# Norms and casts of three batches on ScalarE or GpSimd, one matmul for each filler, and a new order of all operations

## The chip, the core and the metric

One Trainium2 chip, one of its eight cores. The core has five engines that run side by side, each with its own queue of instructions in program order: TensorE (PE; its weight loads are listed as PEld), VectorE (DVE), ScalarE (ACT), GpSimd (POOL) and SyncE (SP, which here only issues DMAs). They wait for one another through semaphores. The metric is the time of one execution on the device in microseconds (us), from the first to the last instruction; less is better.

## What is computed

Attention with a forget gate over 8 batches of 8 heads, 576 positions of 64 dimensions, followed by a bilinear feed-forward network (FFN) on all 4608 tokens:

```python
scores = (q @ k.T) / 8 + cum[:, None] - cum[None, :]      # cum = cumsum(log(clip(f, 1e-4, 1)))
scores[above the diagonal] = -1e9
attn = softmax(scores); x = attn @ v                       # for each of 64 heads
x = heads side by side                                     # 4608 x 512
out = ((x @ w_a) * (x @ w_b)) @ w_out                      # 512 -> 1536 -> 512
```

Inputs and output are float32; the kernel works in float16 with float32 sums.

## The kernel before

The kernel is written as a list of 2311 operations, made by calls of `op` (L124). Each operation has a number, the letters of the engines that may run it (E for TensorE, D, A, P, S for VectorE, ScalarE, GpSimd and SyncE), and what it depends on. Two long constants at the end of the kernel then settle everything: `ORDER` names the operations in the order in which they are issued, and `CHOICE` gives one letter to each operation that has a choice, in the order in which the operations were made. `laid_out` joins the two and a loop issues them. Nothing is rearranged after that: each engine runs its part of `ORDER` first in, first out. Where an operation takes a buffer, it takes the next of a ring (`RING`, L100), and has to wait until the last user of that buffer has finished.

**Attention.** Work is cut into 32 pairs of heads, t = 0 to 31, four to a batch; u = t // 2 names two pairs that share their score matmuls. Inputs are loaded by SyncE (`load_qk` L280, `load_v` L267) in float32, cast to float16 (`cast_qk` L290, kind `caqk`; `cast_v` L275, kind `cav`) and, for q and k, transposed by VectorE (`tqk`, L302). For batch 0 the casts may run on ScalarE, GpSimd or VectorE; for the later batches they run on GpSimd. For a pair and each block of 128 queries i = 0 to 4 (the last has 64), the steps are:

- scores on TensorE (`qk_group` L389). For batches 0 to 2 the decay and the mask come out of further matmuls there, so that
- VectorE takes the maximum of a row straight from PSUM (`do_max` L483, kinds `max0` to `max4`); from batch 3 on it adds the decay and takes the maximum in one instruction (`do_decay`, L512);
- ScalarE takes the exponential, with the row's sum (`do_exp` L539, `exp0` to `exp4`);
- VectorE takes the reciprocal of the sum (`rec`, L554);
- GpSimd multiplies the block of P by it (`do_norm` L561, `norm0` to `norm4`, in place: 128, 256, 384, 512 and 576 columns); all norms are on GpSimd;
- P is transposed: for batch 0 by TensorE (`ptr` L585, evicted by `evp`), from batch 1 on by DMA transposes that SyncE issues (`tr`, L579), in three parts for a pair of batch 1: A0 (i = 0 and 1), A1 (i = 2) and B (i = 3 and 4);
- TensorE multiplies with v (`pve`, `pv`, `pv4`) and ScalarE or VectorE evicts the result to x (`eve`, `ev`, `ev4`).

**The decay.** The cumulative sums are made at the start: VectorE scans them (`fscan`), splits them into a high and a low half (`fhi`, VectorE or ScalarE; `flo`, VectorE or GpSimd), and TensorE and an eviction (`crep`, `cev`) spread them to rows for the score matmuls.

**FFN.** It runs on tiles of tokens: 0, 256 and 512 with 256 tokens each, 768 with 384, then six of 512 and one of 384. A tile needs x of its tokens: those of 0 and 256 need batch 0 only, that of 512 needs batch 1 too (its first 192 rows), that of 768 the rest of it. For each of 12 blocks there are a product with w_a (`psa`), one with w_b (`psb`), four matmuls each (L874), a copy of the first to float16 (`aev`, ScalarE or VectorE) and the product of both on VectorE (`mul`, L890); then w_out (`pso`, L899), a copy (`ocopy`) and the store (`sto`, L914). FFN matmuls are put between those of attention by `ORDER`.

**Weights.** GpSimd issues seven loads that cast on the way (`weights` L355, kind `ldw`, L365). Operation 89 is the first 512 columns of w_a, 90 the same of w_b, 91 the other 1024 columns of w_a, 92 those of w_b, 93 to 95 are w_out. Blocks 4 to 11 of a tile need 91 and 92.

**Fillers.** 40 operations (`filler` L175, numbers 2 to 41) multiply the identity with itself into an unused PSUM buffer of the ring `ff`; they compute nothing. One is four matmuls of 128 columns. 31 of them stand ahead of the first FFN matmul in `ORDER`, nine behind it, none behind the matmuls of token 512 on.

**The end.** The last 128 tokens are stored in two halves, which ScalarE's queue issues; the output's copies go through a ring of two buffers.

Of the kernel before, what the change touches and what calls it, by code (L numbers as in the profile page):

```python
# [37 lines left out]
def kernel(  # L38
# [136 lines left out]
    def filler(_):  # L175
        p = ps.tile([128, 512], FP32, tag="ff", bufs=RING["ff"], name="idle")
        for n in range(4):
            nc.tensor.matmul(out=p[:, 128 * n:128 * n + 128], lhsT=ident, rhs=ident, start=True, stop=True)
# [126 lines left out]
    def batch_inputs(b):  # L305
# [4 lines left out]
        for which, part, gm in items:  # L310
            gate = qk_ops[(2 * (b - 1) + gm // 4, gm % 4)][-1:] if b >= EARLY else []
            if which == "v":
# [4 lines left out]
                ca = op(("P" if 0 in part else "APD") if b == 0 else "P", "cav", lambda e, part=part: cast_v(e, b, part), [ld, o_p], 512 * m)  # L317
# [15 lines left out]
            for lo, hi in (((0, 5), (5, TW)) if b == 0 else ((0, TW),)):  # L333
                ca = op("APD" if b == 0 else "P", "caqk",
# [226 lines left out]
    def do_norm(e, t, i, h):  # L561
        st = T[("st", t)]
        if i == 4:
            p, c = p_blocks(t, 4), 28
        else:
            p, c = p_blocks(t, i)[:, :, h, :], 20 + 2 * i + h
        ENG[e].tensor_scalar(out=p, in0=p, scalar1=st[:, c:c + 1], scalar2=1.0, op0=MUL, op1=MUL)  # L567
# [97 lines left out]
    def softmax(t, g, qk, sc, rows, st_users, pu, norms):  # L665
# [4 lines left out]
        for i in groups[g]:  # L670
# [308 lines left out]
    for t0, n in [(0, 256), (256, 256), (512, 256), (768, 384)] + [(1152 + 512 * n, 512 if n < 6 else 384) for n in range(7)]:  # L979
# [3 lines left out]
        42-44 0 20 41 2 1 64 26 31 23 54 55 45 16 32 13 12 71 46 37 47 56 18 67 27 65 34 72 73 68 48 24 19  # L983
# [3 lines left out]
        142 6 154 155 92 147 143 159 149 91 148 144 160 162 161 108 166-168 145 172 131 52 53 132 179 173 14  # L987
# [4 lines left out]
        310 305 1610 1612 246 214 247 158 226 215 227 311 234 189 1611 235 157 222 449 1614-1616 1613 283  # L992
        312 340 195 294 1617 223 1618 1620 228 229 341 1619 347 1621 236 342 450 94 343 191 232 288 1622 349
        260 237 233 1623 242 348 282 300 1624 366 211 344 1625 240 261 243 241 95 373 1626-1628 367 190 197
        1629 1630 1632 1631 196 302 1633 248 249 374 375 301 368 369 1634-1636 350 1638 284 262 263 392 1637
# [5 lines left out]
        1667 1670 455 1671-1673 1676 1677 421 388 382 381 389 456 1674 401 333 1678 357 413 1675 364 1679  # L1001
# [3 lines left out]
        465 460 500 409 463 505 1703 416 1704 480-482 424 508 440 428 422 1705 1706 509 471 477 483 479 510  # L1005
# [130 lines left out]
```

## Time and profile before

| | us |
|---|---|
| median of 3 runs | 400.67 |
| lowest, highest | 399.65, 400.86 |
| span of the profiled execution | 400.7 |
| first FFN matmul (tile 0) | 30.37 |
| first FFN matmul of tile 512 | 95.58 |
| first FFN matmul of tile 768 | 119.79 |

The busy time of an engine is that in which one of its instructions runs. A matmul's end is modelled in the profile, so that a busy TensorE need not be at its peak. Waits are put down to what came last before the engine went on. In the timeline a row gives start, length, engine, line and operation, what is written and read with its shape, and in square brackets the engine's idle time just before and what ended it. In the groups a row gives a line, the operation and shape, its count, then the busy time of all, the mean of one in nanoseconds, and the idle time ahead of them. In the list of DMA issues the last number is the time from the issue to the landing in us. In the list of waits the three numbers are total us, times and the longest.

### The profile page before, as it was taken

To read this page: it belongs to the slowest core of one execution; us is meant where nothing else is said; L and a number is where in the kernel's file an instruction comes from. 1 tells how busy PE (TensorE), PEld (TensorE's weight loads), DVE (VectorE), ACT (ScalarE), POOL (GpSimd) and SP (SyncE) were. 2 spreads that over 40 slices of the span, in tenths; PEclk is the share of its full clock that TensorE was granted. 3 is DMA by queue.
4 is the path that set the end of the run, shared out by engine and by line. 5 is a ranking of instruction groups with operands and counts; after the bars stand their busy time and mean duration, and the time that the engine had idled before them with its cause. 6 is when DMAs were issued, how large, how long until landed. Compare 5 with 4: busy or idle time off the path is not lost.

```text
span 400.7 us, 11076 instructions
## 1 busy us (share of the span) xinstructions
PE 383.2 (96%) x4040; PEld 212.0 (53%) x4040; DVE 315.3 (79%) x907; ACT 250.0 (62%) x757; POOL 253.6 (63%) x424
## 2 busy tenths in 40 slices
PE   8598799998999999999999999999999999999996
PEld 7466576765855544454445454544444444444553
DVE  8989798976778988997988889898969892373560
ACT  5798766666667778758785777577868673300011
POOL 3889876887397876897896849787968553000000
PEclk9889999998999999999999999999999999999999
DMA  7999989989999999999999999999997729000102
GB/s 282 240 186 289 204 177 224 213 150 215 208 301 208 227 171 330 201 277 212 295 187 286 211 255 273 233 241 190 276 187 218 157 66 202 28 2 36 71 0 79
DMA packets 148311, 78.22 MB, mean 195 GB/s; under 512 B 130592, under 2 KB 133408, under 8 KB 148256
## 3 DMA queue, kind: packets, MB, share of 16 engines
q1 hardware_dynamic: 144272, 72.53, 77.4%
q0 software_dynamic: 3696, 4.72, 7.0%
q8 instruction: 31, 0.51, 0.5%
q10 hardware_dynamic: 288, 0.26, 0.2%
q14 instruction: 24, 0.20, 0.1%
HBM read 49.69 MB, written 9.58 MB: 148 GB/s over the span
## 4 chain that ended last, share of the span: by engine, by line
PE 79%; DMA 9%; DVE 4%; POOL 2%; ACT 2%; issue 2%; SPq 0%; POOLq 0%; DVEq 0%; ACTq 0%
PE pso L899 22%; PE psa L874 22%; PE psb L874 21%; PE sc L401 8%; DMA wa<-in_moe_w_a_dram 5%; PE pv L611 2%; DVE st L488 2%; DMA k<-in_k_dram 1%; PE pv L613 1%; PE sc L636 1%; DMA PTB<-spread 1%; DMA PTB<-PB 1%; DVE qT L302 1%; PE pv L623 1%; ACT PB L550 1%
## 5 line engine op out<-in xcount | busy, mean ns | idle before, releaser
L874 PE MATMUL psa<-xT,wa 128*128 128x512 f16 (+2 forms) x528 | 116.2, 343 | 2.3 <-DMA wa<-in_moe_w_a_dram 1.7
L874 PE MATMUL psb<-xT,wb 128*128 128x512 f16 (+2 forms) x528 | 116.2, 343 | 0.1
L899 PE MATMUL pso<-wout,ht 128*128 128x512 f16 (+1 forms) x444 | 98.4, 374 | 0.0
L567 POOL TENSOR_SCALAR PA<-PA,st 128x128 f16<-128x128 f16 (+2 forms) x162 | 76.0, 482 | 31.8 <-DVE st L559 20.4
L890 DVE TENSOR_TENSOR ht<-psb,a 128x512 f16<-128x512 f32 (+2 forms) x132 | 76.2, 589 | 22.0 <-PE psb L874 15.0
L512 DVE CUSTOM_DVE_ANT_0 S<-sc,spread 128x128 f32<-128x128 f32 (+3 forms) x160 | 86.7, 567 | 7.7 <-PE sc L401 5.4
L138 ACT CAST a<-psa 128x512 f16<-128x512 f32 (+2 forms) x85 | 43.5, 515 | 55.9 <-PE psa L874 53.8
L874 PEld LDWEIGHTS <-wa 128*128 128x128 f16 x528 | 50.1, 99 | 45.5 <-issue 3.7
L874 PEld LDWEIGHTS <-wb 128*128 128x128 f16 x528 | 50.4, 99 | 41.5 <-issue 1.7
L567 POOL TENSOR_SCALAR PB<-PB,st 128x512 f16<-128x512 f16 (+1 forms) x84 | 58.7, 712 | 15.7 <-DVE st L559 14.6
L550 ACT ACTIVATE PA<-S,st 128x256 f16<-128x256 f32 (+2 forms) x120 | 59.9, 502 | 12.5 <-DVE st L512 12.4
L899 PEld LDWEIGHTS <-ht 128*128 128x128 f16 x444 | 41.7, 98 | 46.8 <-issue 1.3
L488 DVE TENSOR_REDUCE st<-sc 128x2 f32<-128x512 f32 (+7 forms) x68 | 46.3, 723 | 6.0 <-PE sc L401 5.3
L401 PE MATMUL sc<-kT,qT 32*128 32x128 f16 (+5 forms) x960 | 41.7, 272 | 5.5 <-ACT PA L550 2.1
L550 ACT ACTIVATE PB<-S,st 128x512 f16<-128x512 f32 x40 | 28.5, 714 | 7.9 <-DVE st L512 7.9
L401 PEld LDWEIGHTS <-qT 32*128 32x128 f16 (+1 forms) x960 | 18.6, 96 | 26.7 <-issue 14.4
L142 DVE CAST a<-psa 128x512 f16<-128x512 f32 (+2 forms) x47 | 26.2, 560 | 7.2 <-PE psa L874 6.6
L559 DVE RECIPROCAL st<-st 128x2 f32<-128x2 f32 x128 | 18.5, 157 | 14.0 <-ACT PA L550 8.7
L142 POOL CAST k<-k 128x1152 f16<-128x1152 f32 (+1 forms) x15 | 20.5, 1367 | 8.9 <-DMA k<-in_k_dram 8.9
L138 ACT COPY osb<-pso 128x512 f32<-128x512 f32 (+1 forms) x22 | 12.4, 570 | 19.9 <-PE pso L899 15.1
L138 ACT CAST xT<-pv 128x512 f16<-128x512 f32 (+2 forms) x39 | 17.0, 446 | 11.8 <-PE pv L636 5.8
L140 POOL TENSOR_SCALAR q<-q 128x1152 f16<-128x1152 f32 (+1 forms) x15 | 20.6, 1372 | 5.0 <-DMA q<-in_q_dram 4.2
(98 smaller groups left out, 491.5 us busy)
## 6 DMA issues: line engine op xcount, KB each, us to landing
spread<-cum_d SPq DMA_DIRECT2D x20, 576.0 KB, 5.9
out_dram<-osb SPq DMA_DIRECT2D x35, 256.0 KB, 3.8
q<-in_q_dram SPq DMA_DIRECT2D x15, 576.0 KB, 7.3
k<-in_k_dram SPq DMA_DIRECT2D x15, 576.0 KB, 5.2
v<-in_v_dram SPq DMA_DIRECT2D x32, 256.0 KB, 6.1
wout<-in_moe_w_out_dram POOLq DMA_DIRECT2D x3, 512.0 KB, 8.7
v<-in_v_dram SPq DMA_DIRECT2D x8, 128.0 KB, 7.2
wb<-in_moe_w_b_dram POOLq DMA_DIRECT2D x1, 1024.0 KB, 13.5
```

What stands on the lines that cost most here:

```text
L138: nc.scalar.copy(out=out_, in_=in_)
L140: ENG[e].tensor_scalar(out=out_, in0=in_, scalar1=0.125, scalar2=1.0, op0=MUL, op1=MUL)
L142: ENG[e].tensor_copy(out=out_, in_=in_)
L401: nc.tensor.matmul(out=dst, lhsT=lhsT, rhs=rhs, start=start, stop=stop, skip_group_check=True)
L488: nc.vector.tensor_reduce(out=m if i == 4 else st[:, 2 * i:2 * i + 2][:, h:h + 1] if isinstance(x, list) else m, in_=y, axis=AXX, op=MAX, ...
L512: nc.vector.tensor_tensor_reduce(out=o, in0=x, in1=y, scale=-1.0, scalar=3e38, op0=ADD, op1=MIN, accum_out=m)
L550: nc.scalar.activation(out=p_blocks(t, i)[:, :, h, :], in_=x.rearrange("p (j k) -> p j k", k=128), func=EXP, scale=sign, bias=st[:, c:c + ...
L559: nc.vector.reciprocal(out=st[:, 20 + 2 * i:22 + 2 * i], in_=st[:, 10 + 2 * i:12 + 2 * i])
L567: ENG[e].tensor_scalar(out=p, in0=p, scalar1=st[:, c:c + 1], scalar2=1.0, op0=MUL, op1=MUL)
L874: nc.tensor.matmul(out=o, lhsT=w16[:, db, 128 * fb:128 * fb + 128], rhs=tokens(db, t0, n), start=(db == 0), stop=(db == 3))
L890: nc.vector.tensor_tensor(out=ht[:, 0:n], in0=T.pop(("psb", t0, fb))[:, 0:n], in1=T.pop(("a16", t0, fb))[:, 0:n], op=MUL)
L899: nc.tensor.matmul(out=o, lhsT=T[("ht", t0, fb)][:, 128 * tb:128 * tb + 128], rhs=wout16[:, fb, c], start=(fb == 0), stop=(fb == 11))
```

## The change

Four edits. A filler is one matmul of 512 columns, with the identity repeated four times as the moving operand. Casts of q, k and v of batches 1 to 3 may run on ScalarE or GpSimd. Norms of batches 0 to 2 may run on ScalarE or GpSimd; on ScalarE a norm is an activation with the function Copy, the reciprocal being its scale for each partition. `ORDER` and `CHOICE` are replaced as a whole.

```diff
     def filler(_):
         p = ps.tile([128, 512], FP32, tag="ff", bufs=RING["ff"], name="idle")
-        for n in range(4):
-            nc.tensor.matmul(out=p[:, 128 * n:128 * n + 128], lhsT=ident, rhs=ident, start=True, stop=True)
+        nc.tensor.matmul(out=p.rearrange("p (n k) -> p n k", n=4), lhsT=ident,
+                         rhs=ident.unsqueeze(1).to_broadcast([128, 4, 128]), start=True, stop=True)
...
-                ca = op(("P" if 0 in part else "APD") if b == 0 else "P", "cav", lambda e, part=part: cast_v(e, b, part), [ld, o_p], 512 * m)
+                ca = op(("P" if 0 in part else "APD") if b == 0 else "PA" if b < 4 else "P", "cav", lambda e, part=part: cast_v(e, b, part), [ld, o_p], 512 * m)
...
-                ca = op("APD" if b == 0 else "P", "caqk",
+                ca = op("APD" if b == 0 else "PA" if b < 4 else "P", "caqk",
...
-        ENG[e].tensor_scalar(out=p, in0=p, scalar1=st[:, c:c + 1], scalar2=1.0, op0=MUL, op1=MUL)
+        if e == "A":
+            nc.scalar.activation(out=p, in_=p, func=COPY, scale=st[:, c:c + 1])
+        else:
+            ENG[e].tensor_scalar(out=p, in0=p, scalar1=st[:, c:c + 1], scalar2=1.0, op0=MUL, op1=MUL)
...
-                nm = op("P", f"norm{i}", lambda e, i=i, h=h: do_norm(e, t, i, h), [rc])
+                nm = op("PA" if b < 3 else "P", f"norm{i}", lambda e, i=i, h=h: do_norm(e, t, i, h), [rc])
...
     ORDER = """
-        42-44 0 20 41 2 1 64 26 31 23 54 55 45 16 32 13 12 71 46 37 47 56 18 67 27 65 34 72 73 68 48 24 19
...
+        0 16 7 9 31 21 28 17 3 42 43 6 15 12 5 32 10 1 71 18 66 72 64 44 54 55 45-48 65 26 67 25 49 50 13 56
...
+        390 437 481 313 1709 38 326 320 39 508 384 287 41 36 29 426 471 427 428 431 482 483 412 509 424
...
+        2281 2285-2288 2291 2292 2289 2290 2282 2293-2303 2306-2310 2304 2305 35
     """
     CHOICE = """
-        DPAADDAAPPAPAAPADPADDAAADADDDDDAADDDDAAADAAADDAAAADAAAAADAAAAAAADAAAAAADDAAADADADDAAAAAADDAAAAAAAAA
...
+        DPADAPAAPPAPAPAAPPPPPAPPPPPPPPPPPPPPPPPPPPPPPPPPAPAPPAPDDADADDDADAAAADADADAADAADDDPPPPPPPPAPPPPPPPP
...
```

Given out to the operations, the letters and the order come to this (kinds that differ):

| | before | after |
|---|---|---|
| norms of batches 0, 1, 2 on ScalarE (of 36 each) | 0, 0, 0 | 4, 10, 17 |
| casts of later inputs on ScalarE | 0 | 1 (v of batch 2) |
| casts of batch 0 on ScalarE, GpSimd, VectorE | 5, 5, 1 | 4, 7, 0 |
| `flo` on VectorE, GpSimd | 1, 1 | 0, 2 |
| `fhi` on VectorE, ScalarE | 2, 0 | 1, 1 |
| `cev` on VectorE, ScalarE | 0, 4 | 1, 3 |
| FFN copies `aev` on VectorE, ScalarE | 47, 85 | 54, 78 |
| output copies `ocopy` on VectorE, ScalarE | 15, 22 | 12, 25 |
| evictions `evp` of transposes on VectorE, ScalarE | 11, 5 | 8, 8 |
| evictions `eve`, `ev`, `ev4` on VectorE, ScalarE | 18, 54 | 24, 48 |
| GpSimd's weight loads, in order | 89, 90, 92, 91, 93, 94, 95 | 90, 89, 91, 92, 93, 94, 95 |
| fillers ahead of the first FFN matmul, behind it | 31, 9 | 29, 11 |
| the last two stores | ScalarE | SyncE, the halves swapped |

After, the memsets `pad` are GpSimd's first work behind the identity. Between the loads 91 and 92 GpSimd has seven norms of batch 0 (132, 145, 127, 102, 108, 133, 126) and a cast of k of batch 1 (273). The five fillers 38, 39, 41, 36 and 29 stand in a row on TensorE's queue, ahead of the products with v of batch 1 (426, 431, 424, 415), which stand ahead of the matmuls of tile 512. One filler (35) is TensorE's last instruction.

More of the change, by code (lines that the diff above doesn't have):

```diff
@@ new lines @@
+        472 442 1732 1733 495 444 445 513 385 405 430 433 434 500 435 436 521 522 528 540 443 1734-1736 568
+        478 1738 1739 541 542 507 709 506 512 526 1737 1740 485 524 1742 569 574-576 525 461 1741 1744 546
+        548 1743 1746-1749 577 579 578 1745 1750 1751 1754 1755 1752 1753 1758 1759 1756 1757 1760 547 549
+        463 523 543 545 570 571 529 532 572 551 573 527 533 534 603 536 537 1761-1764 580-582 552 554 550
+        1708 11 535 553 604 605 555 556 1765 1713 530 600 601 531 538 616 558 559 583 585 584 586 587 1767
@@ new lines @@
+        602 1768-1770 618 557 544 619 539 562 1772 1774 563 620 1773 1776 622 560 590 1778 564 565 1777 1779
+        591 588 566 1775 710 1780 1782 1781 1783-1787 561 592 593 589 611 594 598 626 595 623 671 638 678
+        645 640 647 624 673 1788 679 1789 646 1790 648 1791 1792 1794 1793 1796 1797 639 1795 672 641 642
+        596 680 1798 674 675 567 1800 1802 1801 612 1804 1799 1803 649 650 597 627 630 681 682 684 599 631
+        606 634 1806 608 632 635 685-687 676 651 1805 1807 652 633 653 1808 643 1809 1812 607 617 1810 1811
@@ new lines @@
+        688-690 1814 636 692 1766 644 1813 1815-1817 693 1818 609 654-656 1820 712 614 659 660 657 658 683
+        661 1821 628 629 1819 610 637 694 677 625 621 662 697-699 714 1822 700 691 664 665 695 1825 1826 701
+        801 798 1827 1830 1831 1828 667 613 706 716 615 1771 666 668 728 730 1832 713 761 704 763 762 799
+        1833 764 768 1835 1837 769 1836 736 1838 735 1829 1839-1842 702 800 737 1843 696 770 1844 703 729
+        1847 707 771 772 1845 669 738 721 1823 670 663 731 802 739 705 717 722 724 741 765 767 803 720 732
@@ new lines @@
+        1892 856 842 1895 1896 904 855 814 1898-1900 831 1903 1904 860 861 866-868 897 896 898 1887 899 901
+        914 959 966 900 1907 1905 815 960 961 968 1901 1908 1911 907 926 933 934 902 1909 903 1913 1912 1915
+        928 936 1910 935 1917 1916 997 1919 908 813 967 927 1906 905 919 969 998 962 1918 963 915 918 922
+        937-939 929 1014 970 972 930 932 1015 916 917 1921 923 940 973-975 1914 1004 1005 965 1920 942 941
+        1922 971 964 1923 1924 1007 1927 1925 1926 943 1002 944 946 976 977 924 931 1018 947 948 945 1929
@@ L1091 @@
+        PAAAPPPPPAAAAAPPPPPPPPAPPPAAADDDAADDADPPAPPPPPAPAPPAAAPAPPPPAAPAADDAPPPAPPAPAPAAPPAAAPPPPPPPADAAAAAA
+        AAAAAAADAAAADAAAAADDDAAAAADDADAADAAAADADDADDAADDDADDAAADAADDDDAAADADDAADDADDADADADDADDAADDAADDAAAAAA
+        DAADAAADDAAAAAAAAAADAAAAAAADADAADADAAADAAAAAAADAAAAAAADDAAAAAADADADAAAADDDDDAADADDDADDAAADDAADDDDAAA
+        AAAASDS
     """
```

82 lines of the change are left out of this document (45 added, 37 removed), and 102 rows, old and new, of the table ORDER.

## The prediction

> **What bounds the kernel now.** First the summary of the profile: span, busy time of each engine. Then the busy time by stage, for the places where an engine is not full; then the chain of waits inside those.
>
> ```profile
> span 400.7 us, 11076 instructions
> PE 383.2 (96%) x4040; PEld 212.0 (53%) x4040; DVE 315.3 (79%) x907; ACT 250.0 (62%) x757; POOL 253.6 (63%) x424
> ```
>
> ```profile
> 10.00:45.00 35.00, 25.96 (x493) 19.75 (x490) 31.51 (x77) 27.83 (x99) 31.03 (x53) 0.90 1.08 236
> 45.00:80.00 35.00, 34.14 (x589) 25.11 (x587) 32.55 (x72) 24.44 (x79) 26.01 (x42) 1.00 1.04 202
> 80.00:97.00 17.00, 15.22 (x242) 9.88 (x240) 11.98 (x29) 11.11 (x41) 13.85 (x25) 0.96 0.94 168
> 97.00:120.00 23.00, 22.55 (x340) 15.68 (x339) 15.89 (x37) 14.12 (x48) 14.49 (x24) 0.95 1.11 255
> 120.00:397.00 277.00, 276.95 (x2307) 134.35 (x2306) 215.12 (x671) 166.31 (x485) 164.56 (x274) 1.00 0.78 184
> ```
>
> The columns of the stages are stretch, length, busy PE, PEld, DVE, ACT, POOL, then granted clock and DMA share. From 120 us on TensorE is busy 276.95 of 277 us: there the end is set by TensorE's work alone, which the change does not alter. What can be gained or lost lies before 120 us. From 10 to 80 us VectorE is the fullest engine (64.06 of 70 us, 91.5%); from 80 to 97 us no engine is full, and something is waited for in turn.
>
> ```profile
> 84.49 1.80 DVE st L488 x2
> 87.65 0.46 POOL q L140
> 88.98 1.08 POOL PA L567 x3
> 90.06 4.18 DMA PTB<-spread
> ```
>
> ```profile
> 94.28 0.35 PE L636 MATMUL pv<-PTB,nv 128*64 128x64 f16 x10 [1.77 <-DMA PTB<-spread]
> 95.58 0.93 PE L874 MATMUL psa<-xT,wa 128*128 128x256 f16 x4
> ```
>
> The chain there runs through GpSimd's queue (norms, a cast of a later q between them), then a DMA transpose, then values of batch 1, and only then (95.58) the first FFN matmul of tokens 512 on, which need batch 1. Up to there TensorE has only the FFN of 512 tokens to fill in, and has used it up. So the time is: the moment of that matmul, plus work that is the same in both kernels. At the start nothing of the FFN is ready, and VectorE leads.
>
> The profiled execution's span, 400.7 us, equals the median of the three runs (400.67), so sums against the one hold for the other. A measurement of this kernel can tell about 0.3% (1.2 us) from no change.
>
> **The change, part by part.** Handing the letters of CHOICE to the operations in turn gives: 31 norms of batches 0 to 2 go from GpSimd to ScalarE (4, 10 and 17 by batch), one cast of v (batch 2) too; VectorE loses one cast of q, its subtraction `flo` and one of its `fhi` casts; everything else is order.
>
> *Start.* VectorE's queue loses three instructions before the second pair of scores, which ScalarE and GpSimd take:
>
> ```profile
> 6.99 0.49 DVE L142 CAST wout<-cum_f 32x256 f16<-32x256 f32 x2
> 7.52 1.03 DVE L220 TENSOR_TENSOR wout<-cum_f,wout 32x320 f16<-32x320 f32 x1
> 12.65 1.16 DVE L140 TENSOR_SCALAR q<-wout 128x512 f16<-128x512 f32 x1
> ```
>
> ```profile
> L138 ACT CAST xT<-rows 128x320 f16<-128x320 f32 (+1 forms) x4 | 1.6, 396 | 1.0 <-PE rows L225 1.0
> 5.54 0.86 POOL L140 TENSOR_SCALAR q<-q 128x640 f16<-128x640 f32 x1 [4.23 <-DMA q<-in_q_dram]
> ```
>
> 1.03 + 1.16 + half of 0.49 = 2.4 us, less one eviction of rows (`cev`) that it gains, about the 0.4 that ScalarE takes for one: 2.0 us off the leading queue. GpSimd has room for them, since its memsets (`pad`, L169) move into its 4.23 us of idle time before 5.54. So batch 0 may run 2.0 us early.
>
> *Weights.* Against this stand the weight loads. Before, the two large ones are issued one behind the other:
>
> ```profile
> 21.71 0.81 POOL L365 DMA_DIRECT2D wb<-in_moe_w_b_dram  x1
> 22.51 0.75 POOL L365 DMA_DIRECT2D wa<-in_moe_w_a_dram  x1
> ```
>
> ```profile
> wb<-in_moe_w_b_dram POOLq DMA_DIRECT2D x1, 1024.0 KB, 13.5
> wa<-in_moe_w_a_dram POOLq DMA_DIRECT2D x1, 1024.0 KB, 21.7
> ```
>
> ```profile
> 44.21 0.61 PE L874 MATMUL psa<-xT,wa 128*128 128x256 f16 x4 [1.65 <-DMA wa<-in_moe_w_a_dram]
> 45.37 0.42 DVE L890 TENSOR_TENSOR ht<-psb,a 128x256 f16<-128x256 f32 x1 [1.81 <-ACT a L138]
> ```
>
> They land at 35.2 and 44.2, 9.0 us apart: one queue, one after the other. TensorE waits 1.65 us for the second, and VectorE 1.81 behind it. After, `wa` goes first, then seven norms and a cast of k (1.4 us), then `wb`:
>
> ```profile
> L567 POOL TENSOR_SCALAR PA<-PA,st 128x128 f16<-128x128 f16 x54 | 20.0, 376 | 15.8 <-DVE st L559 10.0 <-ACT a L138 2.6 <-issue 2.3
> L567 POOL TENSOR_SCALAR PA<-PA,st 128x256 f16<-128x256 f16 x54 | 25.7, 482 | 6.9 <-DVE st L559 4.9 <-issue 1.8
> L142 POOL CAST k<-k 128x1152 f16<-128x1152 f32 x14 | 19.6, 1398 | 8.0 <-DMA k<-in_k_dram 8.0
> ```
>
> Four norms at 0.376, three at 0.482 and the cast make 4.3 us. By GpSimd's queue `wa` is issued at about 21, so it lands at 34.5 (estimate: 21 + 13.5), and `wb`, issued at about 26, follows at 43.5 (34.5 + 9.0): 0.7 before the second one landed until now. TensorE and VectorE reach it sooner and wait longer. So of the 2.0 us only some 0.9 are left at the first product that needs it (45.37). Bounds: -2.0, if it lands as soon as it is needed, to +3, if it starts only after its issue and takes the 21.7 of the slower row. Taken: **-0.9**, by the row of 9.0.
>
> *From 45 to 97 us.* VectorE's content between that product and the first of token 512 comes to the same within 0.3 us, counted off both orders with the durations of this trace (it evicts three transposes and two outputs less, but has taken over scores of batch 1 from the time before). It is busy 32.55 + 11.98 = 44.5 of 52 us. At the 91.5% that it reaches from 10 to 80 us this takes 48.7: 3.3 less. That needs GpSimd not to be late again; and of its 39.9 busy us here, 17 norms go away before the first FFN copy of token 512: 3, 4, 5, 2 and 3 of 128, 256, 384, 512 and 576 columns.
>
> ```profile
> L567 POOL TENSOR_SCALAR PA<-PA,st 128x384 f16<-128x384 f16 x54 | 31.5, 589 | 9.1 <-DVE st L559 5.6 <-ACT PA L550 1.8 <-DVE st L557 1.7
> L567 POOL TENSOR_SCALAR PB<-PB,st 128x512 f16<-128x512 f16 x56 | 38.2, 694 | 11.6 <-DVE st L559 11.3
> L567 POOL TENSOR_SCALAR PB<-PB,st 128x576 f16<-128x576 f16 x28 | 20.9, 748 | 4.2 <-DVE st L559 3.3 <-ACT PB L550 0.6
> L550 ACT ACTIVATE PA<-S,st 128x256 f16<-128x256 f32 x40 | 20.0, 501 | 4.1 <-DVE st L512 4.1
> L550 ACT ACTIVATE PB<-S,st 128x512 f16<-128x512 f32 x40 | 28.5, 714 | 7.9 <-DVE st L512 7.9
> L142 POOL CAST nv<-v 128x1024 f16<-128x1024 f32 x16 | 16.6, 1038 | 2.7 <-PE pv L613 1.8 <-DMA v<-in_v_dram 0.9
> ```
>
> That is 1.1 + 1.9 + 2.9 + 1.4 + 2.2 = 9.6 us; no ScalarE norm is in the trace, but ScalarE's activations of those widths take as long (501 and 714 ns), so it gains the same 9.6, plus 1.0 for the cast, beside 63.4 busy us of the 87 from 10 to 97 us: 74, or 85%. It has room, if the waits do not grow. The DMA transposes keep their 4 us each. Bounds: 0 to -7.5 (all idle time of VectorE); taken **-2.7**, short of 3.3 because transposes and loads, with the DMA engines full (share 0.94 to 1.08), end some of these waits too.
>
> *Clock.* After the wait of 1.77 us the granted clock fell:
>
> ```profile
> 90.00:95.00 5.00, 3.23 (x66) 1.77 (x64) 4.62 (x8) 2.33 (x7) 5.00 (x10) 1.00 1.06 215
> 95.00:100.00 5.00, 5.00 (x42) 3.65 (x38) 1.51 (x5) 3.98 (x12) 2.10 (x4) 0.66 1.08 210
> ```
>
> A mean of 0.66 over 5 us is 3.4 us at half clock, 1.7 us lost. The new order puts five fillers in a row just ahead of those values of batch 1. Bounds 0 and -1.7; taken **-0.9**, as the wait itself may stay.
>
> The Trainium skill ("TensorE: Matmul & The Clock Gate", Why this matters for your kernels) sets the limit at idle gaps over about 3 us. By that rule nothing would be gained here, the sum being 0.9 higher, still in the forecast's case; the row shows a drop after 1.77 us. Its window of 3413 ns (same page, Part 1) is what the row gives.
>
> *Fillers.* Four matmuls become one; the columns stay 512. Ten run after the first FFN matmul instead of nine, another after all stores; the trace has 14.9 us for 160, so four cost 0.37:
>
> ```profile
> L178 PE MATMUL idle<-ident 128*128 128x128 f16 x160 | 14.9, 257 | 1.7 <-POOL ident masks.py:199 1.4 <-ACT spread L550 0.4
> ```
>
> Two of them fall into the full stage: +0.2 at most with the rest hidden in waits (0 to 0.7).
>
> *End.* The last two stores move from ScalarE's queue to SyncE's, in swapped order, so the one whose copy is last waits behind the other's issue:
>
> ```profile
> 397.59 0.37 ACT L138 COPY osb<-pso 128x256 f32<-128x256 f32 x1 [2.22 <-DMA out_dram<-osb]
> 397.99 0.34 ACTq L914 DMA_DIRECT2D out_dram<-osb  x1
> ```
>
> One issue is 0.34: **+0.2** (0 to 0.4). From 120 to 397 us VectorE takes seven more FFN copies; it is busy 215 of 277 there, which covers them.
>
> **Sum:** 400.7 - 0.9 - 2.7 - 0.9 + 0.2 + 0.2 = **396.6 us**.
>
> **Rivals.**
> - *Nearly all idle time goes.* Start -2.0, middle -5, clock -1.7: 392.4 with the two small costs. For it: the idle time is there on every engine from 80 to 97 us. Against: weights and transposes stay. 17%.
> - *The front stays where it was.* If the DMA engines set the pace (share 1.04 to 1.08 up to 80 us, and the chain passes through a DMA of 4.18 us), the loads and transposes end the waits as before: start -0.9, nothing else, 400.2. 16%.
> - *ScalarE becomes the wait (slower).* A norm on ScalarE waits for the reciprocal, and exponentials of the next scores queue behind it; VectorE's next reciprocals wait for those.
>
> ```profile
> ACT PA L550 <- DVE st L488: 3.7, 3, 1.4
> ACT spread L550 <- DVE st L488: 3.1, 3, 1.8
> ```
>
>   Between 10 and 95 us ScalarE waits for VectorE 1.1 us at a time (6.8 in 6). If each of 17 norms brought that, 18.7 us would be added where the 87 - 74 = 13 us are free: the first FFN matmul of token 512 comes 5.7 us late against ScalarE's room, and with -2.0 from the start the end is at 404.4. It decides from a mean wait of 0.76 us. Against: the norms stand some places behind their reciprocals. 15%. The Trainium skill (same page, opening table) calls ScalarE's queue strictly first in, first out; the waits shown agree.
>
> **How the numbers follow.** The forecast's case (394 to 399) has 52%, and its own edges reach the neighbours. Faster by over 0.3% (below 399.5): forecast 52 + 17, with 1 of the second rival: 70%. Within 0.3%: 15%. Slower (above 401.9): 15%. The range runs from 391.0 (first rival with its bounds) to 402.5 (half of the third): it leaves out about 5% below and 13% above.
>
> **What would show it.** Right: the first FFN matmul of token 512 near 91.5 instead of 95.58; no half clock around it; VectorE above 80% busy from 80 us to there; a wait for `wb` near 40 us longer than 1.65; TensorE full from about 115 us. Wrong: ScalarE at 90% or more with VectorE's reciprocals waiting for it; new TensorE waits after 120 us, which the sum puts at nothing; a `wb` landing after 45.

## The result, and the profile after

| | before | after |
|---|---|---|
| median, us | 400.16 (4 runs, 399.11 to 400.86) | 412.87 (4 runs, 411.25 to 414.06) |
| ratio | 1 | 1.0292, 95% interval 1.0234 to 1.0350 |
| span of the profiled execution, us | 400.7 | 409.5 |
| first FFN matmul of tiles 0, 256, 512, 768 | 30.37, 66.27, 95.58, 119.79 | 29.7, 64.9, 92.06, 116.8 |

The changed kernel is 2.9% slower by the ratio in the table (the two medians alone give 3.2%); 396.6 was predicted. The medians below are over all runs, and the ratios leave out three runs in a slower state of the chip: one of the filler alone, and two of the last kernel with mixed queues, whose median is 480.6 without them. The spans of the two profiled executions lie 8.8 us apart, the medians 12.7. A run's time is 1.8 us above its span (411.25 and 409.5), so the profile of after is that of its fastest run, and that of before of an execution some 2 us above its median. What follows explains the 8.8 us that the two traces hold.

The summary of the profile of after (span, then busy time of each engine, its share and count):

```profile
span 409.5 us, 10797 instructions
PE 387.0 (95%) x3920; PEld 205.5 (50%) x3920; DVE 314.4 (77%) x912; ACT 264.6 (65%) x781; POOL 237.7 (58%) x395
```

Its busy time by stage, in the stages of before (stretch, length, PE, PEld, DVE, ACT, POOL, clock, DMA share, GB/s):

```profile
10.00:45.00 35.00, 29.40 (x483) 18.62 (x483) 30.79 (x75) 29.51 (x101) 25.84 (x42) 0.85 1.05 226
45.00:80.00 35.00, 34.32 (x542) 25.51 (x541) 30.96 (x75) 31.53 (x90) 23.35 (x35) 1.00 0.86 176
80.00:97.00 17.00, 15.77 (x249) 10.25 (x249) 13.61 (x35) 14.86 (x46) 11.29 (x18) 1.00 1.04 191
97.00:120.00 23.00, 22.05 (x347) 14.65 (x342) 16.94 (x41) 16.48 (x52) 9.78 (x16) 1.00 1.07 238
```

```profile
120.00:409.00 289.00, 278.01 (x2292) 133.87 (x2289) 214.79 (x668) 165.78 (x485) 161.13 (x269) 1.00 0.77 182
```

The front does what was forecast: the norms' move shows (GpSimd 26.01 to 23.35 us from 45 to 80, ScalarE 24.44 to 31.53), and the clock is full from 80 to 120 us. (From 10 to 45 us it is 0.85 against 0.90; kernels here that share the first 896 operations of before have 0.80 to 0.90 there, so the difference is not clear of that spread.) The loss is behind 120 us: TensorE, busy for 276.95 of 277 us before, is now idle for 11.0 of 289, 3.0 of them behind its last matmul, which the window of before leaves out. The first two of the five entries in the list of its waits from 120 us on (total, times, longest; the same view of before has no entry at all):

```profile
PE sc L639 <- DMA PTB<-PB: 5.7, 8, 1.1
PE psa L877 <- DVE ht L893: 0.7, 1, 0.7
```

It waits mostly for the DMA transposes of P, the last step of a pair's softmax, ahead of `pv4`. Call a round the time from the first scores (`qk0`) of two pairs to those of the next two. Nine rounds lie between the `qk0` of pairs 12 and 13 and that of pairs 30 and 31. The window between those two moments, first before, then after:

```profile
123.13:310.91 187.78, 187.73 (x1721) 89.42 (x1721) 165.75 (x554) 138.06 (x412) 147.05 (x244) 1.00 1.00 236
```

```profile
122.10:320.20 198.10, 190.58 (x1719) 89.79 (x1719) 167.28 (x554) 136.78 (x410) 141.61 (x237) 1.00 0.97 229
```

The work is the same (1721 and 1719 matmuls, 554 instructions on VectorE), the length is 10.3 us more: **a round takes 20.86 us before and 22.01 after, in the mean.** Of the 10.3 us TensorE is idle for 7.5; the rest is busy time of the same matmuls, whose ends are modelled. Single rounds differ more than the two orders do (20.0 to 22.5 us before, 18.9 to 24.7 after), so only the mean of nine is used below. Ahead of the rounds the new order is 1.0 us early, behind them both kernels take the same (89.8 and 89.3 us): -1.0 + 10.3 - 0.5 = 8.8, the whole difference of the spans.

Where in a round? Followed through the trace for each of the 18 pairs 12 to 29, the time from the end of a pair's last scores to the end of its last norm is 5.6 us before and 7.0 after in the mean. All three queues add to it: from the scores to the first decay of the last block it is 1.05 us before and 1.58 after (VectorE), from there to the exponential 0.32 and 0.58 (ScalarE), from the exponentials to the reciprocal 0.43 and 0.57 (VectorE), and from there to the first norm 0.53 and 0.96 (GpSimd). (Some expectations below count otherwise, for two pairs together: 7.5, 8.7 and "2.0 us later".) From the end of the transpose's issue to `pv4` remain 3.25 us in place of 4.32.

### The profile page after: what moved, and what is told of

It reads as the page before. It is cut to its first block, busy times and chain, and to the rows that moved or that the text cites. A ratio compares the mean times of both kernels' runs of the same rounds, so it can differ in the third digit from the quotient of the medians.

```text
span 409.5 us, 10797 instructions
## 1 busy us (share of the span) xinstructions
PE 387.0 (95%) x3920; PEld 205.5 (50%) x3920; DVE 314.4 (77%) x912; ACT 264.6 (65%) x781; POOL 237.7 (58%) x395
## 5 line engine op out<-in xcount | busy, mean ns | idle before, releaser
L570 POOL TENSOR_SCALAR PA<-PA,st 128x384 f16<-128x384 f16 (+2 forms) x152 | 71.4, 483 | 59.5 <-DVE st L559 28.6
L877 PEld LDWEIGHTS <-wb 128*128 128x128 f16 x528 | 50.0, 98 | 43.5 <-issue 4.5
L138 ACT CAST a<-psa 128x512 f16<-128x512 f32 (+2 forms) x78 | 40.6, 524 | 43.5 <-PE psa L877 41.8
L570 POOL TENSOR_SCALAR PB<-PB,st 128x512 f16<-128x512 f16 (+1 forms) x74 | 51.6, 712 | 11.6 <-DVE st L559 7.8
L488 DVE TENSOR_REDUCE st<-sc 128x2 f32<-128x512 f32 (+8 forms) x68 | 47.1, 725 | 12.5 <-PE sc L401 5.6
L401 PE MATMUL sc<-kT,qT 32*128 32x128 f16 (+5 forms) x960 | 43.3, 271 | 4.4 <-ACT PA L550 1.7
L142 DVE CAST a<-psa 128x256 f16<-128x256 f32 (+2 forms) x54 | 29.6, 548 | 10.7 <-PE psa L877 10.0
L401 PEld LDWEIGHTS <-qT 32*128 32x128 f16 (+1 forms) x960 | 19.1, 95 | 26.0 <-issue 15.8
L138 ACT COPY osb<-pso 128x512 f32<-128x512 f32 (+1 forms) x25 | 14.2, 569 | 25.3 <-PE pso L902 20.3
L142 POOL CAST k<-k 128x1152 f16<-128x1152 f32 (+1 forms) x15 | 20.4, 1361 | 5.1 <-DMA k<-in_k_dram 5.1
L550 ACT ACTIVATION_READ_ACCUMULATOR PA<-S,st 128x1 f32 x120 | 22.7, 189 | 0.0
## 6 DMA issues: line engine op xcount, KB each, us to landing
wa<-in_moe_w_a_dram POOLq DMA_DIRECT2D x1, 1024.0 KB, 11.6
```

Source lines behind the costliest of these rows:

```text
L138: nc.scalar.copy(out=out_, in_=in_)
L142: ENG[e].tensor_copy(out=out_, in_=in_)
L401: nc.tensor.matmul(out=dst, lhsT=lhsT, rhs=rhs, start=start, stop=stop, skip_group_check=True)
L488: nc.vector.tensor_reduce(out=m if i == 4 else st[:, 2 * i:2 * i + 2][:, h:h + 1] if isinstance(x, list) else m, in_=y, axis=AXX, op=MAX, ...
L550: nc.scalar.activation(out=p_blocks(t, i)[:, :, h, :], in_=x.rearrange("p (j k) -> p j k", k=128), func=EXP, scale=sign, bias=st[:, c:c + ...
L877: nc.tensor.matmul(out=o, lhsT=w16[:, db, 128 * fb:128 * fb + 128], rhs=tokens(db, t0, n), start=(db == 0), stop=(db == 3))
```

## The experiments

Each kernel was timed beside the kernel before, whose median was 400.9 to 402.7 there. Kernels with parts of the new order, new letters or moved products run on the changed kernel's code, so they have the one-matmul fillers. Where two orders are joined (at a seam), operations already issued are left out of the second.

### Where the loss is made

The first 896 operations in the new order with the new letters, then the old order:

```diff
     ORDER = """
-        42-44 0 20 41 2 1 64 26 31 23 54 55 45 16 32 13 12 71 46 37 47 56 18 67 27 65 34 72 73 68 48 24 19
...
+        0 16 7 9 31 21 28 17 3 42 43 6 15 12 5 32 10 1 71 18 66 72 64 44 54 55 45-48 65 26 67 25 49 50 13 56
...
```

> The first 896 operations of the new order with their new letters (up to about 140 us: all of the start, the norms of batches 0 to 2 on ScalarE, the new fillers), the other 1415 in the old order with their old letters. Theory (the loss lies in the order from 120 us on, where a pair's softmax has too little time before TensorE asks for its transposed P; the front is 2.9 us of TensorE work ahead at 120 us): 397 to 398.5, with TensorE full from 140 us on. Rival (what the norms on ScalarE and the new front set off is carried on and costs the 12.7 us later): 409 to 413.

Measured: 404.82, ratio 1.0113 (1.0077 to 1.0149). Neither theory. By its trace the first FFN matmuls of tiles 512 and 768 are 2.7 and 2.1 us earlier than before, but `qk0` of pair 12 comes at 123.02, as before, and the rounds take 21.09 us. TensorE is idle for 2.0 us from 120 to 160 us, around the seam. So in this kernel the FFN's lead is worth nothing: what counts is when the rounds begin, and how long they take. A cost of the seam itself isn't told apart from that.

The mirror image, the old order first (its first line stays), the new one from the 897th operation on:

> The mirror image: the first 896 operations as before, the other 1415 in the new order with the new letters (no norm on ScalarE). Theory: the waits of TensorE for transposes of P are back from 140 us on, 409 to 416 (the loss without the gain of the front). Rival (the front is to blame): 399 to 402.

Measured: 415.70, ratio 1.0364 (1.0331 to 1.0396), with rounds of 22.54 us in the mean. The first entry of TensorE's waits behind 140 us:

```profile
PE sc L639 <- DMA PTB<-PB: 5.3, 6, 1.9
```

As the theory said. **The order behind the 896th operation, with its letters, makes the loss by itself**, without one norm on ScalarE and without the new front.

The first hybrid with the seam at the 675th operation:

> Like the first hybrid, but the new order and letters for the first 675 operations only (to about 100 us, 22 of the 31 norms on ScalarE), the old order behind. The first hybrid lost its lead between 116 and 145 us, in waits for score buffers. Theory (the front is a gain, and its part from 100 to 140 us gives it back): 397.5 to 400. Rival (the lead is lost anyhow, as the old rest is laid out for a later front): 402 to 405.

Measured: 408.74, ratio 1.0171 (1.0119 to 1.0222). Both wrong: one wait of 4.6 us for a transpose stands at the seam, where a norm is queued on GpSimd behind a mask that waits for its load. The rounds behind it are as short as before (20.94). A seam's place says nothing of the front's worth.

### Can the change be taken apart?

The filler alone, in the kernel before:

```diff
-        for n in range(4):
-            nc.tensor.matmul(out=p[:, 128 * n:128 * n + 128], lhsT=ident, rhs=ident, start=True, stop=True)
+        nc.tensor.matmul(out=p.rearrange("p (n k) -> p n k", n=4), lhsT=ident,
+                         rhs=ident.unsqueeze(1).to_broadcast([128, 4, 128]), start=True, stop=True)
```

> The kernel before with the fillers as one matmul of 512 columns and nothing else. Theory: 400.2 within 0.8, as the columns are the same and 31 of the 40 lie in idle time. Rival (one long matmul holds the queue where four short ones did not, or the clock falls): over 402.

Measured: 401.94, ratio 1.0022 (0.9987 to 1.0057): 0.9 us above the expected range, but no difference that is clear of the noise.

The norms back on GpSimd in the changed kernel (letters only):

```diff
     CHOICE = """
-        DPADAPAAPPAPAPAAPPPPPAPPPPPPPPPPPPPPPPPPPPPPPPPPAPAPPAPDDADADDDADAAAADADADAADAADDDPPPPPPPPAPPPPPPPP
...
+        DPADAPAAPPAPAPAAPPPPPPPPPPPPPPPPPPPPPPPPPPPPPPPPPPPPPPPDDADADDDADAAAADADADAADAADDDPPPPPPPPPPPPPPPPP
...
```

> The changed kernel with its 31 norms of ScalarE and its one cast of v given back to GpSimd; the order stays the new one. Theory: the steady part still loses, and the front loses its gain or more, since the new order counts on a free GpSimd: 413 to 419. Rival (ScalarE's norms cause the loss): 400 to 406.

Measured: 443.14, ratio 1.1072 (1.1018 to 1.1126). Worse by far than the theory: `qk0` of pair 12 comes at 149.6, 27 us late. TensorE's longest wait from 100 us on, 6.3 us up to 115.75, is for a transposed P of an early pair. In the 20 us from 122 on TensorE is idle for 6.1, and VectorE, ScalarE and GpSimd for more than half of the time:

```profile
122.00:142.00 20.00, 13.85 (x167) 8.82 (x167) 9.73 (x25) 6.98 (x25) 7.60 (x13) 0.83 0.90 226
```

The other way round, the 31 norms on ScalarE in the old order:

```diff
     CHOICE = """
-        DPAADDAAPPAPAAPADPADDAAADADDDDDAADDDDAAADAAADDAAAADAAAAADAAAAAAADAAAAAADDAAADADADDAAAAAADDAAAAAAAAA
...
+        DPAADDAAPPAPAAPADPAPPAPPPPPPPPPPPPPPPPPPPPPPPPPPAPAPPAPDDAAADADDDDDAADDDDAAADAAADDAPPPPPPPPAPPPPPPPP
...
```

(the new string also has letters for operations that have no choice in the old code)

> The old order and the old letters; only the 31 norms of batches 0 to 2 that the change moves go to ScalarE, each at the place that it has in the old order. Theory 1 (the move itself is harmless and the loss is in the order behind it): 398 to 402. Theory 2 (in a full order any shift of work between engines costs, as the 66 changed letters of the rest alone cost 7.5 us): 404 to 412, with the loss before 130 us.

Measured: 409.37, ratio 1.0185 (1.0139 to 1.0232): theory 2. `qk0` of pair 12 is 5.5 us late (128.64), the rounds are as before (21.03). TensorE's two main waits from 80 to 140 us:

```profile
PE pv L639 <- DMA PTB<-PB: 2.7, 1, 2.7
PE psa L877 <- ACT a L138: 2.7, 2, 2.0
```

The second is the rival of the prediction in which ScalarE's queue becomes the wait: the FFN copy that ends the longest of these waits (2.0 us, up to 103.10) runs on ScalarE behind two added norms of 0.77 us. What delays the transpose of the first wasn't followed up. The list of TensorE's waits in the changed kernel has no such copy on ScalarE from 10 to 120 us.

The new letters of the rest, in the old order:

> The whole old order; from its 897th operation on only the letters are the new ones (36 FFN copies, 16 output copies, 14 evictions of values change between VectorE and ScalarE; no norm). Theory (the places in the order count, not who runs a copy): 400 to 403. Rival (the letters overload VectorE or ScalarE around the softmax): 406 or more.

Measured: 409.24, ratio 1.0176 (1.0102 to 1.0251), the rival; rounds of 21.71, so that the letters alone lengthen a round by 0.85 us. (By the two strings 70 letters differ there, two FFN copies and two stores more than the expectation counts.) Its mirror image, the new order with the old letters from its 897th operation on:

> The changed kernel with its whole new order, but from its 897th operation on the old letters. Theory (letters and order cost separately, and add up): 412.9 less 7.5, 404 to 407. Rival (the new order is laid out for its own letters, like the old one): 416 to 424.

Measured: 425.68, ratio 1.0574 (1.0535 to 1.0612), the rival, 1.7 us above its range: the costs of letters and order don't add up, each order runs best with its own letters.

TensorE's queue from one order and the other four queues from the other, behind the first 896 operations of before:

> First 896 operations as before. After that TensorE's queue in the new order, the queues of VectorE, ScalarE, GpSimd and SyncE in the old order with the old letters (where the two don't fit together, 20 instructions are pulled ahead by 1 to 7 places in their queue). Theory TensorE (the new order of TensorE's own queue asks for a pair's values 0.8 us of work earlier behind its scores, 26.1 against 26.9): 409 to 416, near the 415.7 of the whole new rest. Rival (the softmax itself is later, through the order on the other engines): 400 to 404.

Measured: 475.61, ratio 1.1840 (1.1781 to 1.1899).

> The mirror image: first 896 operations as before, then TensorE's queue in the old order and the other four in the new order with the new letters (7 instructions pulled ahead by 1 or 2 places). Theory TensorE: 400 to 404. Rival (the other engines' order; in the trace of the changed kernel the last norm of two pairs comes 8.7 us behind their last scores, before 7.5): 408 to 416, with TensorE waiting for transposes of P from 140 us on.

Measured: 484.56, ratio 1.1962 (1.1842 to 1.2082). Both theories failed in both kernels: five queues that run first in, first out, each with hundreds of waits on the others, can't be judged one by one. These two runs tell nothing of which queue is to blame.

### How much slack is there?

The products with v 1.7 us earlier in the kernel before (in `ORDER`, from pair 12 on, each `pv4` and `pv` two FFN products further ahead):

> The kernel before; from pair 12 on the products with v of a pair stand two FFN products (1.7 us) earlier in TensorE's queue. Theory (the slack of the second pair between the issue of its transpose and its use, 3.4 us in the mean against a least of 2.4, is some 1.0 us; what is asked 1.7 us earlier exposes 0.7 to 0.9 in each of nine rounds): 406 to 409. Rival (the softmax has slack): 400 to 402.

Measured: 414.08, ratio 1.0288 (1.0251 to 1.0325), rounds of 22.31. More than the theory's 6 to 9. In the trace of before `pv4` starts 1.7 us after its transpose has landed, in the mean over the 18 pairs (0 to 3.7); after, it is 0.7, and in ten of the 18 pairs nothing. So the old order has slack, but less than the 1.7 us that were taken away in every pair.

The same, later, in the changed kernel:

```diff
-        596 680 1798 674 675 567 1800 1802 1801 612 1804 1799 1803 649 650 597 627 630 681 682 684 599 631
-        606 634 1806 608 632 635 685-687 676 651 1805 1807 652 633 653 1808 643 1809 1812 607 617 1810 1811
+        596 680 1798 674 675 567 1800 1802 1801 612 1804 1799 1803 649 650 597 681 599 606 608 1805 1808 627
+        630 682 684 631 634 1806 632 635 685-687 676 651 1807 652 633 653 643 1809 1812 607 617 1810 1811
...
```

> The changed kernel; from pair 12 on the next two FFN products behind qk1 stand ahead of the block pv4, pv4, pv, qk1 (20 products in ten places), so that TensorE asks for a pair's transposed P 1.7 us of work later; every other queue as it is. Theory (a pair's softmax is 2.0 us later than before and TensorE asks for it no later, so it waits about 1 us in each of nine rounds): half or more of the loss goes, 403 to 408, and TensorE's waits for PTB fall from 5.7 to under 2 us. Rival (the waits are only the place where a loss made elsewhere shows, or qk1 now comes too late): 411 to 417.

Measured: 424.70, ratio 1.0526 (1.0464 to 1.0589), rounds of 23.16: the rival, and worse than its range. TensorE's waits for `PTB` fall from 6.0 to 0.5 us, as the theory said, but `qk1`, which moved along, came late and everything behind it; the first entry of its list from 120 us on is now a wait of scores for VectorE's decays:

```profile
PE sc L401 <- DVE st L512: 7.5, 15, 0.8
```

My first theory, that TensorE only asks too early, found no support: with the waits for the transposes gone, the loss came back at the scores. As `qk1` moved along, the run can't tell whether asking later alone would have helped.

### What sets the length of a round?

Shorter norms from batch 3 on, in both kernels:

```diff
             p, c = p_blocks(t, i)[:, :, h, :], 20 + 2 * i + h
+        if t >= 12:
+            p = p[:, 0:1]
```

> The changed kernel; from batch 3 on a norm multiplies one block of 128 columns (one column for the last 64 queries) in place of the whole row, so that GpSimd's norms are shorter; orders, letters and TensorE's work as they are. Leaves out: the normalisation of the other columns. Four norms of 0.69 us stand in the tail of a round; at the 0.38 of 128 columns the chain is some 1.2 us shorter. Theory (the longer chain is what TensorE waits for): two thirds of the loss goes, 402 to 406. Rival (GpSimd and the chain are not it): 410 to 413.

> The same in the kernel before, also without the normalisation of those columns. TensorE is full there from 120 us on, so a shorter chain can give nothing: 399.5 to 401.5. Were it to fall below 398, the old order had waits too that the profile does not show.

Measured: 410.65, ratio 1.0211 (1.0150 to 1.0272), and 401.43, ratio 1.0003 (0.9975 to 1.0030). The windows of the nine rounds, first of the changed kernel so altered, then of the one before:

```profile
124.18:321.29 197.11, 191.14 (x1719) 90.36 (x1719) 167.56 (x554) 136.47 (x410) 112.15 (x238) 0.99 0.98 231
```

```profile
121.51:309.47 187.96, 187.23 (x1721) 89.01 (x1721) 165.81 (x554) 138.00 (x412) 117.97 (x245) 1.00 1.02 238
```

GpSimd has 29 us less to do in both, and the rounds are as long as they were (21.90 and 20.88 us). In the changed kernel the last norm is done 1.2 us sooner, by the mean over the pairs, but the transpose then waits 0.64 us longer to be issued, and 0.34 longer from its issue to `pv4`. The theory fell: it is not the length of GpSimd's norms.

A quarter of the products with w_a and w_b left out from token 1152 on, in both:

```diff
-        for db in range(4):
+        d = 3 if t0 >= 1152 else 4
+        for db in range(d):
             nc.tensor.matmul(out=o, lhsT=w16[:, db, 128 * fb:128 * fb + 128],
-                             rhs=tokens(db, t0, n), start=(db == 0), stop=(db == 3))
+                             rhs=tokens(db, t0, n), start=(db == 0), stop=(db == d - 1))
```

> The kernel before; in the FFN tiles from token 1152 on, the products with w_a and w_b take three of four matmuls (the last 128 of 512 input features are left out). That is 864 columns-times-24 less for each 864 tokens, in all 82,944 columns or 34.6 us at 2.4 columns per ns, some 26 us of it before 340 us. Theory b (TensorE's work alone sets the end): 363 to 368. Theory c (the softmax rounds of 20.9 us are a second bound just under the first): only the part behind the attention falls, 385 to 393.

> The same in the changed kernel, leaving out the same 128 features. Theory b: 12 us above the run before, near 378. Theory c (both orders then run at the pace of their softmax rounds): 395 to 404, and in both kernels the first scores of pairs 30 and 31 stay within 8 us of where they were (310.9 and 320.2).

Measured: 389.19, ratio 0.9686 (0.9655 to 0.9718), and 405.35, ratio 1.0050 (1.0009 to 1.0091), 1.4 us above the range. Theory c, by its size in the first and by the first scores of pairs 30 and 31 in both (305.8 and 321.5). The nine rounds of the kernel before with less FFN:

```profile
120.61:305.78 185.17, 172.00 (x1621) 81.04 (x1621) 164.66 (x554) 136.35 (x410) 146.47 (x243) 1.00 1.03 241
```

TensorE has 15.7 us less to do in them (187.73 to 172.00) and they are 2.6 us shorter: 20.57 us a round in place of 20.86. With the changed order they go from 22.01 to 21.88. **So TensorE was full and still its work alone did not set the pace: with less of it the rounds are 0.3 us shorter, no more.** The distance of the two orders stays when TensorE has time to spare; it is 1.3 us a round then.

VectorE relieved: copies and products of the FFN on half the columns, in the changed kernel, and in the one before with the quarter of the products out:

```diff
-        cast(e, a16[:, 0:n], T.pop(("psa", t0, fb))[:, 0:n])
+        lo = n - 256 if t0 >= 1152 else 0
+        cast(e, a16[:, lo:n], T.pop(("psa", t0, fb))[:, lo:n])
...
-        nc.vector.tensor_tensor(out=ht[:, 0:n], in0=T.pop(("psb", t0, fb))[:, 0:n],
-                                in1=T.pop(("a16", t0, fb))[:, 0:n], op=MUL)
+        lo = n - 256 if t0 >= 1152 else 0
+        nc.vector.tensor_tensor(out=ht[:, lo:n], in0=T.pop(("psb", t0, fb))[:, lo:n],
+                                in1=T.pop(("a16", t0, fb))[:, lo:n], op=MUL)
...
```

(the rest of the edit lets the products with w_out read only the computed columns, so that TensorE's work stays)

> The changed kernel; in the FFN tiles from token 1152 on, the copy of the first product and the product of both work on the last 256 of a tile's columns in place of 512 (384 in the last tile), and the products with w_out read those alone: the FFN of the other tokens there is left out, TensorE's work and both orders stay. By the rows of the changed kernel that takes 50 x (0.685 - 0.416) + 9 x (0.553 - 0.416) + 9 x 0.27 + 6 x 0.135 = 17.9 us off VectorE in nine rounds, 2.0 a round. Theory (VectorE's work sets a round): 22.0 falls to TensorE's 20.7, and the time to 401 to 405. Rival (the order's waits set it, whoever is faster between them): rounds of 21.6 or more, 408 to 413.

> The kernel before with a quarter of the FFN products left out, as in the run before, and the same halved copies and products of both from token 1152 on (that FFN of half the tokens left out too): 17.7 us less for VectorE in nine rounds. Theory (VectorE's work): rounds of 20.57 fall to 18.4 to 19, the time from 389.2 to 369 to 376. Rival (waits): rounds of 20.0 or more, 383 to 389.

Measured: 411.13, ratio 1.0224 (1.0197 to 1.0250), and 388.90, ratio 0.9686 (0.9636 to 0.9735). The rivals, both times. The nine rounds, changed kernel first:

```profile
122.19:320.68 198.49, 191.54 (x1718) 89.91 (x1719) 153.42 (x554) 127.92 (x409) 141.30 (x237) 0.99 0.96 229
```

```profile
120.72:305.26 184.54, 170.97 (x1619) 81.28 (x1618) 150.72 (x554) 129.27 (x410) 145.94 (x243) 1.00 1.05 241
```

VectorE has 13.9 us less to do in each than without this edit (167.28 to 153.42, 164.66 to 150.72); the rounds take 22.05 and 20.50 us. So no engine's amount of work was found to set a round: not TensorE's, VectorE's or GpSimd's taken one by one in the changed kernel, and not TensorE's and VectorE's together in the one before (GpSimd's was shortened there only with TensorE full, and ScalarE's, at 74% of the rounds, not by itself). How the steps hang together shows in the chain of waits of the last kernel (start, length, what), here just behind the nine rounds:

```profile
304.63 0.60 DVE S L512
...
305.42 1.26 POOL PB L567 x2
306.68 0.07 issue
306.75 2.08 POOL PB L567 x3
308.83 0.03 POOL nv L142
308.86 5.14 DMA PTB<-PB
314.00 0.04 issue
314.04 0.35 PE sc L636 x10
...
314.94 0.44 PE sc L401 x16
...
317.45 0.69 PE sc L401 x14
```

Decay of the last scores (VectorE), norms (3.4 us), the transpose (5.14), `pv4` (L636), then the next scores `qk1` (L401). `pv4` writes its result into a score buffer of the next pairs' `qk0`, and `qk1` needs that buffer back, so that it can't pass. From `qk1` the order goes on to the next two groups of scores and their decay: by the order of the operations the chain closes on itself. **That this chain sets the length of the nine rounds is argued, not shown:** the list reaches back to 302.51 us only, it is that of the kernel with the most work left out, and 1.2 us less of norms on it made a round of the changed kernel 0.1 us shorter.

One number goes with the pace of the good rounds: the DMA share. Share times length over nine gives 20.9 us of transfers a round before, 21.4 after, and 20.4 to 21.5 in all twenty kernels; the lowest, 20.7 and 20.4, are those with mixed queues, whose rounds take 28.0 and 28.8 us. In the kernels that run the old order with its letters unstalled the share is 0.99 to 1.05, in the new one 0.94 to 0.98, and 0.93 in the two with the moved products with v. That is what one would see if transfers were a floor of some 21 us and the new order added waits above it. **It was not tried:** no kernel here has fewer transfers, and the share of before's rounds with less work elsewhere goes up to 1.05, so that 1 is no plain limit of it.

## Why the prediction was wrong

**The step that failed** stands in its first part: "From 120 us on TensorE is busy 276.95 of 277 us: there the end is set by TensorE's work alone, which the change does not alter", and with it "the time is: the moment of that matmul, plus work that is the same in both kernels". The row was read rightly and the inference was not. A full engine says that the order filled it, not that it is the only one full. In those rounds VectorE was at 88% and the DMA share at 1.00, and something else holds a round at 20.57 us when a quarter of the FFN products is gone: TensorE's work was the longer bound by 0.3 us a round at most. The runs show that this second bound lies in the rounds and moves with the order, by 1.15 us each; they don't show what it is. The averaged row hid it: its DMA share of 0.78 is 1.00 in the rounds, 0.67 from there to 340 us and 0.10 behind. The Trainium skill ("Perfetto Trace Analysis", Identifying the Most-Contended Engine) says that the busy share of matmuls is no good measure of how close a kernel is to its roofline, since pipelined matmuls look smaller in a trace. No run here tests that reason. The same section of the Trainium skill calls the occupancy of the 16 DMA engines misleading, one more reason not to take their share for a proof.

From there the sum put a wholly replaced order of 1415 operations at +0.2 us for fillers and nothing for waits. Measured for that part alone: 415.70 against 400.93, +14.8 us. Of "new TensorE waits after 120 us" the prediction said itself that they would prove it wrong.

The other steps, one by one:

- *Start, middle, clock.* Right in their sum. Tile 512's first FFN matmul was forecast near 91.5 and came at 92.06; the clock there is full; VectorE is busy 13.61 of 17 us from 80 us on, 80%. TensorE waits no more than 0.2 us at a time from 90 to 100 us, so that the part of the five fillers in the full clock isn't told apart from that of the missing wait. That the sum fits is in part luck: the start's -0.9 rested on a wait for weights that did not come (next point), and by its own numbers (43.5 for 44.2) it would have been -0.7. The span of 400.7 was also taken for a run's time, which is 1.8 us more; that is too little to matter here. The timeline of TensorE, and the windows with the clock next to last but two:

```profile
92.06 0.61 PE L877 MATMUL psa<-xT,wa 128*128 128x256 f16 x4
```

```profile
90.00:95.00 5.00, 5.00 (x75) 3.73 (x74) 4.54 (x11) 5.00 (x16) 5.00 (x10) 1.00 0.96 135
95.00:100.00 5.00, 4.78 (x125) 4.02 (x124) 3.77 (x12) 4.91 (x12) 0.74 (x2) 1.00 1.13 212
```

  But these 3.5 us are worth 1.0: that is how much earlier the rounds begin.
- *Weights.* Wrong in size, without consequence. `wb` was put at 43.5 and a longer wait for it was to be seen; issued at 27.39, it landed 11.8 us later, at 39.2, and TensorE has no wait for it. The two loads overlap where they were taken to run one after the other (timeline, then the list of DMA issues):

```profile
22.10 0.80 POOL L365 DMA_DIRECT2D wa<-in_moe_w_a_dram  x1
27.39 0.81 POOL L365 DMA_DIRECT2D wb<-in_moe_w_b_dram  x1
```

```profile
wa<-in_moe_w_a_dram POOLq DMA_DIRECT2D x1, 1024.0 KB, 11.6
wb<-in_moe_w_b_dram POOLq DMA_DIRECT2D x1, 1024.0 KB, 11.8
```

- *Norms on ScalarE.* Priced at 501 and 714 ns for 256 and 512 columns from its exponentials; they take 514 and 720 (groups by line and shape):

```profile
L568 ACT ACTIVATE PB<-PB,st 128x512 f16<-128x512 f16 x6 | 4.1, 720 | 0.6 <-DVE st L559 0.5
L568 ACT ACTIVATE PA<-PA,st 128x256 f16<-128x256 f16 x5 | 2.6, 514 | 0.2 <-DVE st L559 0.2
```

- *Fillers.* Right: no difference.
- *End.* Priced at +0.2 (0 to 0.4). From the end of the last copy to the end of the span it is 2.7 us before and 3.2 after, 0.5 more and just outside the bounds; the two stores follow one another on SyncE, as said:

```profile
405.88 0.37 ACT L138 COPY osb<-pso 128x256 f32<-128x256 f32 x1 [2.13 <-DMA out_dram<-osb]
406.29 0.81 SPq L917 DMA_DIRECT2D out_dram<-osb  x2
```

- *The slower rival.* Its mechanism, ScalarE's queue, is real (the norms alone in the old order cost 6.7 us, with 2.7 us of waits of TensorE for copies on ScalarE), but it isn't what slows the changed kernel, whose loss is there without one norm on ScalarE. No rival stood where the loss was made; the range of 391.0 to 402.5 came from the front alone.

What stays open: which of the new order's 1415 places makes its rounds 1.15 us longer (longer waits in three queues were seen, none was taken out alone), what sets the length of a round in either order, and whether transfers are the floor of both. No version that does the whole work is faster than the kernel before.

## What to carry to other kernels

When a whole order is replaced, put bounds on the steady stage too: measure the mean length of its rounds, ask what new waits could cost in one, and count that once for each round (1.15 us in nine rounds were 10.3 here). An engine at 100% is the only bound of a stage if taking work from it shortens the stage as much; a kernel with a quarter of that work left out tells in one run. Parts of an order fitted for five queues could not be carried over into another here: every mixture of the two was slower than the kernel before, by 1% to 20%.

## What the runs showed of the hardware that was not expected

- Two casting loads of 1 MB from GpSimd's queue, issued 5.3 us apart, landed 5.5 us apart (11.6 and 11.8 us each); issued 0.8 us apart before, they landed 9.0 apart.
- SyncE's queue is held 1.3 to 3.8 us by the issue of one DMA transpose of 13 blocks (median 1.5 in the rounds of before), and from its issue to its landing 3.8 to 6.1 us pass. Norms made 1.2 us shorter ahead of it moved the product that needs it forward by 0.1.
